# Placing every on-chip tile that TensorE reads at a multiple of 128 bytes

## The chip, the cores and the metric

The kernel runs on one core of a Trainium2 chip. The metric is device time in microseconds (us); lower is better. Names of engines in the profile: PE is TensorE's matmul stream, PEld its weight loads, DVE is VectorE, ACT is ScalarE, POOL is GpSimd, SP is the engine that issues nearly all DMAs here.

## What is computed

Talking-heads attention over 8 batches, 12 heads, 448 tokens and head size 64, then a feed-forward layer over 3584 tokens with 768 inputs, 2048 hidden values and 768 outputs. All of it is in fp32; the weights of the second part arrive as float64.

```python
scores = scale * np.matmul(q, k.transpose(0, 1, 3, 2))
scores = np.einsum('bhij,hg->bgij', scores, w_pre)
attn = np.exp(scores - np.max(scores, axis=-1, keepdims=True))
attn = attn / (np.sum(attn, axis=-1, keepdims=True) + 1e-09)
attn = np.einsum('bhij,hg->bgij', attn, w_post)
x = np.matmul(attn, v)          # then heads are joined: 3584 x 768
h = x @ w_in
out = (h - np.tanh(h)) @ w_out
```

## The kernel before

**Two stages.** The first stage is attention. It goes over 32 blocks (8 batches, each of three times 120 tokens and once 88) and over 180 places; a place handles two groups of up to 10 tokens by 12 heads, so 120 rows. At each place `gather` (L487) brings two groups of scores from the tile `s` into tiles `t` by DMA, `split` makes a high and a low float32r part of one group (`th` on DVE at L495, `tl` on POOL at L496), `premix` multiplies by the 120x120 matrix `wpre` (L503, fp32, shown as two records) or by its two parts `wph` and `wpl` (L506 to L508, float32r), `expo` takes maximum and exponential (L518 on DVE, L520 on ACT), `norm` scales `wpost` by the row sums into `wr` (L536 on ACT), and `mix` multiplies the exponentials `e` as weights by `wr` as moving operand (L548), which ACT copies into `at` (L557, L564). Beside this, at places that a small planner picks, `prep_q` transposes queries (L432) and writes them as `qh` on ACT (L445) and `ql` on DVE (L447), `prep_k` does the same for keys (`kk`), `scores` multiplies the two (L466) and `values` multiplies `at` by the values `vr` (L585). The feed-forward weights are narrowed from float64 in the same stage.

The second stage is the feed-forward layer: 7 batches of 512 tokens by 16 slices of 128 hidden values, 112 steps. A step has 18 matmuls of 512 columns in `hidden` (L246, L247, L251: a 128x128 piece of `w` as weights, `xh` or `xl` as moving operand), and for each of four token tiles 3 matmuls of 512 and 3 of 256 columns in `result` (L290, L291, L293: a 128x128 piece of `gh` or `gl` as weights, `w` as moving operand). ACT and DVE do the gate (`gate`, L261 to L271) and its two parts (L278, L279). Weights come through a ring of six tiles, `w0` to `w2` in a pool on the left and `w3` to `w5` in one on the right.

**What sets the order.** Each engine's instructions stand in the order in which the Python code emits them (`in_order`); `sooner`, `then` and `last` put the copies of a place behind its matmuls.

**Where tiles lie.** Pools are stacked from the left end of on-chip memory upwards and from the right end downwards, and every tile starts at a multiple of 32 bytes. No tile is placed by hand, so a small tile moves all that is stacked behind it. With this kernel the left stack of the first stage begins at a multiple of 128, and the two buffers of `qh` and of `ql` (2880 bytes a partition each) break it by 64; the right stack is 96 bytes past a multiple of 128 throughout, since the small tiles of `cst` and the ring of `wr` (960 bytes a buffer) are no whole multiples; and in the second stage the 8-byte tile `bias` puts all that lies behind it on the left 32 bytes past. First bytes, modulo 128, of what TensorE reads:

| read at | moving operand | weights |
|---|---|---|
| L246, L247, L251 | `xh`, `xl`: 0 | `w0` to `w2`: 32; `w3` to `w5`: 96 |
| L290, L291, L293 | `w0` to `w2`: 32; `w3` to `w5`: 96 | `gh`, `gl`: 32 |
| L466 | `kk`: 0 | `qh`, `ql`: 0, 32, 64 and 96, by head pair and buffer |
| L503 | `t`: 96 | `wpre`: 96 |
| L506, L507, L508 | `th`, `tl`: 96 | `wph`: 32, `wpl`: 0 |
| L548 | `wr`: 0, 32, 64, 96 | `e`: 96, 32 |
| L585 | `at`: 0, 32, 64, 96 | `vr`: 96 |
| L406, L432 | `ident`: 96 | `ko`, `qr`: 0 |

Of the kernel before, what the change touches and what calls it, by code (L numbers as in the profile page):

```python
# [10 lines left out]
F32 = mybir.dt.float32  # L11
F32R = mybir.dt.float32r
# [9 lines left out]
def raw(ap):  # L22

    return ap.bitcast(F32)
# [5 lines left out]


CW = 512


def narrow_steps(nc, pool, dma, chunks):
# [5 lines left out]
    def load(src):  # L41
        p, n2 = src.shape
        r = pool.tile([p, CW, 2], I32, name="cr", tag="cr", bufs=3)[:, : n2 // 2]
        return r, dma(r.rearrange("p n t -> p (n t)"), src)
# [23 lines left out]
def narrow_chunk(nc, pool, dma, r, dst):  # L68
    p, n, _ = r.shape
    hi, lo = r[:, :, 1], r[:, :, 0]  # L70
    m = pool.tile([p, CW], F32, name="cm", tag="cm", bufs=2)[:, :n]
    s = pool.tile([p, CW], I32, name="cs", tag="cs", bufs=2)[:, :n]
    u, w = hi, lo
# [23 lines left out]
    fh = s.bitcast(F32R)  # L97
    fl = pool.tile([p, CW], F32R, name="cl", tag="cl", bufs=2)[:, :n]
    nc.scalar.copy(fh, m)
# [46 lines left out]
def kernel_body(  # L146
# [11 lines left out]
    nc = tc.nc  # L158
    B, H, S, D = q.shape
    P = 128  # L160
    DM = H * D
    DF = w_in.shape[1]
    NP = H // 2
# [3 lines left out]
    MT = GI * H  # L167
    GP = GI * H
# [32 lines left out]
    ff = SimpleNamespace(w={}, x={}, raw={}, out={})  # L201

    def open_early():
        def pool(name, bufs):
            return ctx.enter_context(tc.tile_pool(name=name, bufs=bufs, side="left", reuse_waits="tile"))

        ff.xp, ff.w0 = pool("xp", 2 * NK), pool("w0", 1)
        ff.rw, ff.gp = pool("rw", 1), pool("gpool", 3)
        ff.bias = ff.w0.tile([P, 2], F32, name="bias", tag="bias")
        nc.gpsimd.memset(ff.bias[:, 0:1], GATE_A[1])  # L210
        nc.gpsimd.memset(ff.bias[:, 1:2], GATE_B[1])

    def open_ps_h():
        ff.ps_h = ctx.enter_context(tc.tile_pool(name="ps_h", bufs=2, space=PSUM, side="left"))

    def open_late():
        ff.wp = ctx.enter_context(tc.tile_pool(name="wp", bufs=1, side="right", reuse_waits="tile"))
        ff.op = ctx.enter_context(tc.tile_pool(name="op", bufs=4, side="right", reuse_waits="tile"))
        ff.ps_y = ctx.enter_context(tc.tile_pool(name="ps_y", bufs=1, space=PSUM, side="left"))
# [100 lines left out]
    with ExitStack() as st:  # L320

        early, early_ps = ctx.enter_context(ExitStack()), ctx.enter_context(ExitStack())
        ld = early.enter_context(tc.tile_pool(name="ld", bufs=2, side="left"))
        sp = early.enter_context(tc.tile_pool(name="sp", bufs=2, side="left"))
        cv = early.enter_context(tc.tile_pool(name="cv", bufs=1, side="left"))
        cst = st.enter_context(tc.tile_pool(name="cst", bufs=1, side="right"))
        kp = st.enter_context(tc.tile_pool(name="kp", bufs=1, side="right"))
        gp = st.enter_context(tc.tile_pool(name="gp", bufs=4, side="right"))
# [95 lines left out]
        def prep_q(i, t):  # L424

            n = sizes[blocks[i][1]]
            assert sent[i, "q"]()
            ps = ps_m.tile([P, 512], F32, name="ps_m", tag="ps_m")
            pv = ps[:, : 3 * MT].rearrange("p (r i) -> p r i", r=3)
            for r in range(3):  # L430
                hp = 3 * t + r
                nc.tensor.transpose(  # L432
                    pv[:, r, :n], qrs[i][:n, 2 * hp : 2 * hp + 2, :].rearrange("p h d -> p (h d)"), ident[:n, :n]
                )
            pv = pv[:, :, :n]

            def rest():
                if t == 0:
                    qbs[i] = [
                        ld.tile([P, NP * MT], F32R, name=x, tag=x)[:, : NP * n].rearrange("p (h i) -> p h i", i=n)  # L440
                        for x in ("qh", "ql")
                    ]
                qh, ql = qbs[i]
                tt = slice(3 * t, 3 * t + 3)
                nc.scalar.mul(qh[:, tt], pv, scale)  # L445
                then.append(
                    lambda: nc.vector.scalar_tensor_tensor(  # L447
                        out=ql[:, tt], in0=pv, scalar=scale, in1=raw(qh[:, tt]), op0=ALU.mult, op1=ALU.subtract
                    )
                )  # L450
                if t == 1:
                    del qrs[i]

            sooner.append(rest)

        def scores(i, hp, engines=None):
# [68 lines left out]

        def norm(p):
            zs = te[p][1]
            wr = gp.tile([GP, 2, GP], F32, name="wr", tag="wr", bufs=2)
            n0, n1 = rows[2 * p], rows[2 * p + 1]
            for j, n in enumerate((n0, n1)):  # L530

                nc.vector.tensor_scalar_add(zs[:n, 1, j : j + 1], zs[:n, 0, j : j + 1], 1e-9)
            for js, n in ((slice(0, 2), n0),) if n0 == n1 else ((slice(0, 1), n0), (slice(1, 2), n1)):
                nc.vector.reciprocal(zs[:n, 2, js], zs[:n, 1, js])
            for j, n in enumerate((n0, n1)):
                nc.scalar.mul(wr[:n, j, :], wpost[:n, :], zs[:n, 2, j : j + 1])  # L536
            te[p].append(wr)
# [120 lines left out]
        )  # L658
        ps_w = ps_s[:GP, 1, : 2 * H].rearrange("p (w g) -> p w g", w=2)
        nc.tensor.matmul(ps_w.rearrange("p w g -> p (w g)"), repeat, w12.rearrange("p w g -> p (w g)"), start=True, stop=True)  # L660
        wpre = cst.tile([GP, GP], F32, name="wpre")
        wpost = cst.tile([GP, GP], F32, name="wpost")
        pre_v = wpre.rearrange("p (i g) -> p i g", i=GI)
        post_v = wpost.rearrange("p (g i) -> p g i", i=GI)
        nc.vector.tensor_copy(pre_v, ps_w[:, 0, :].unsqueeze(1).to_broadcast([GP, GI, H]))
# [12 lines left out]
        def scores_0(hq):  # L678
            for hp in (2 * hq, 2 * hq + 1):
                scores(0, hp, (nc.scalar.copy, nc.vector.tensor_copy))  # L680
                sooner.pop()()
# [9 lines left out]
        prep_q(1, 1)  # L691
        flush()
        scores_0(2)
        wph = cst.tile([GP, GP], F32R, name="wph")
        wpl = cst.tile([GP, GP], F32R, name="wpl")
        nc.vector.tensor_copy(wph, wpre)
        nc.vector.tensor_sub(wpl, wpre, raw(wph))
        now()
# [35 lines left out]
        at_s, p, kind = {}, 0, None  # L734
        while halved:
            ready = sorted((x for x in halved if x[0] <= p), key=lambda x: (x[1], x[3:]))
            if ready:
                x = ready[0]
# [3 lines left out]
                if x[2] == kind and other and x[1] > p + 1:  # L742
                    x = other[0]
                halved.remove(x)
                _, _, kind, i, n = x
# [7 lines left out]
        for i, (b, m) in enumerate(blocks):  # L753
            p0 = first[i] // 2
            if i + 2 < len(blocks):
                p = at_s[i + 2, 0] - 1
# [7 lines left out]
        for b in range(1, B):  # L764
            p, o = first[blocks.index((b - 1, 1))] // 2 - 1, 0
            for hq in range(3):
                at_place(p, load_k, b, hq)
                p = o = max(p + 2, o)
# [26 lines left out]
        for p in range(NPL + 3):  # L795
# [13 lines left out]
            if 1 <= p < NPL + 1:  # L809
                norm(p - 1)  # L810
# [20 lines left out]
            if p == NPL - 3:  # L831
                conv.rest(now)
                early.close()
                open_early()
# [6 lines left out]


    open_late()
    ahead = RING - 1
    for n in range(EARLY, ahead):
# [53 lines left out]
```

## Time and profile before

| what | value |
|---|---|
| median of three timed runs | 1901.55 us (1899.92 to 1905.39) |
| the profiled execution | 1894.16 us, of which the span of its instructions is 1892.4 us |
| PEld busy | 1528.4 us, 81% |
| DVE busy | 1191.6 us, 63% |
| ACT busy | 1138.7 us, 60% |
| POOL busy | 484.0 us, 26% |
| DMA | 371.92 MB at 197 GB/s on average |
| TensorE clock granted | 0.997 of full speed |

The profile is of one execution, which was 7.4 us under the median of the timed runs. A matmul's record begins when it is issued; its end is modelled, and records of neighbouring matmuls overlap. So the time that a matmul takes in a full stream is read from the distance between the beginnings of neighbouring records, not from the duration in a record. An fp32 matmul has two records, a float32r matmul has one, and a transpose one. A group's row gives the line, engine, operation, tiles and shapes, then its count, its busy time and the mean duration of one, and the idle time before it with what ended it.

### The profile page before, as it was taken

The page shows a single profiled execution, that of the slowest core. Times are in us where ns is not written, and L with a number is a line of the kernel's source. Part 1 is how long each engine was busy: PE and PEld are TensorE (multiplying, and loading weights), DVE is VectorE, ACT ScalarE, POOL GpSimd, SP SyncE. Part 2 cuts the span into 40 slices and gives each one's busy share as a digit, 9 for nine tenths or more (in the row PEclk, how much of TensorE's full clock was granted, in tenths as well). Part 3 has the DMA queues.
Part 4 walks back from the last instruction along what each step waited for, and adds up shares of the span by engine and source line. Part 5 has one row for each costly group of instructions (what it writes and reads, how often), then busy time and mean ns, then how long its engine had stood idle before and what let it go on. Part 6 is the DMA issues. An engine that isn't in the chain of part 4 may idle for free.

```text
span 1892.4 us, 35415 instructions
## 1 busy us (share of the span) xinstructions
PE 1864.3 (99%) x13154; PEld 1528.4 (81%) x13154; DVE 1191.6 (63%) x2464; ACT 1138.7 (60%) x2513; POOL 484.0 (26%) x442
## 2 busy tenths in 40 slices
PE   7999999999999999999999999999999999999998
PEld 5787887877888788787788888888888888888887
DVE  4676766777776686776455565555555555556555
ACT  4887888878888688888634434444444443443433
POOL 1454545444554355544200000010000000010000
PEclk9999999999999999999999999999999999999999
DMA  5567658675665757656565555655656655555550
GB/s 137 181 192 211 189 159 235 180 213 181 195 213 156 208 178 206 204 159 183 194 268 207 210 212 212 226 200 214 218 199 217 215 207 209 212 213 201 214 197 34
DMA packets 199963, 371.92 MB, mean 197 GB/s; under 512 B 55920, under 2 KB 174704, under 8 KB 185456
## 3 DMA queue, kind: packets, MB, share of 16 engines
q1 hardware_dynamic: 199744, 369.67, 59.5%
q8 instruction: 104, 1.70, 0.4%
q14 instruction: 67, 0.55, 0.1%
q10 hardware_dynamic: 48, 0.00, 0.0%
HBM read 245.37 MB, written 47.19 MB: 155 GB/s over the span
## 4 chain that ended last, share of the span: by engine, by line
PE 88%; DMA 5%; ACT 2%; DVE 2%; issue 1%; POOL 1%; SPq 1%; ACTq 0%; POOLq 0%; DVEq 0%
PE ps_o L548 14%; PE ps_h L251 8%; PE ps_h L247 8%; PE ps_h L246 8%; PE ps_m L585 7%; PE ps_q L466 6%; PE ps_p L503 6%; PE ya L290 5%; PE ya L291 5%; PE ya L293 5%; PE yb L291 3%; PE yb L293 3%; PE yb L290 3%; DMA t<-s 2%; PE ps_p L508 2%; PE ps_p L507 2%
## 5 line engine op out<-in xcount | busy, mean ns | idle before, releaser
L548 PEld LDWEIGHTS ps_o<-wr,e 120*112 120x112 f32 (+1 forms) x2880 | 307.6, 177 | 48.7 <-issue 30.6
L548 PE MATMUL ps_o<-wr,e 120*112 120x120 f32 (+1 forms) x2880 | 340.7, 272 | 4.1 <-ACT wr L536 4.1
L518 DVE TENSOR_REDUCE mx<-ps_p 120x1 f32<-120x448 f32 x360 | 218.6, 622 | 134.3 <-PE ps_p L503 134.0
L278 ACT CAST gh<-r 128x512 fp32r<-128x512 f32 (+1 forms) x113 | 69.7, 617 | 381.7 <-DVE r L271 381.7
L496 POOL TENSOR_TENSOR tl<-t,th 120x448 fp32r<-120x448 f32 (+1 forms) x180 | 206.2, 1146 | 355.8 <-DVE th L495 221.3
L247 PE MATMUL ps_h<-xl,w 128*128 128x512 f32 x672 | 266.2, 396 | 0.5 <-POOL xl L236 0.5
L246 PE MATMUL ps_h<-xh,w 128*128 128x512 f32 x672 | 266.1, 396 | 0.0
L236 POOL TENSOR_TENSOR xl<-rx,xh 128x512 fp32r<-128x512 f32 x38 | 57.7, 1519 | 745.8 <-ACT xh L235 745.8
L520 ACT ACTIVATE e<-ps_p,mx 120x448 f32<-120x448 f32 x360 | 226.0, 637 | 31.6 <-DVE mx L518 31.3
L557 ACT COPY at<-ps_o 112x960 f32<-112x960 f32 x156 | 154.6, 991 | 108.2 <-PE ps_o L548 107.5
L290 PE MATMUL ya<-w,gh 128*128 128x512 f32 x448 | 177.4, 396 | 2.5 <-ACT gh L278 2.5
L267 DVE SCALAR_TENSOR_TENSOR r<-qa,ps_h 128x512 f32<-128x512 f32 (+1 forms) x113 | 77.2, 684 | 159.9 <-ACT t L264 159.9
L291 PE MATMUL ya<-w,gh 128*128 128x512 f32 x448 | 177.1, 395 | 0.0
L293 PE MATMUL ya<-w,gl 128*128 128x512 f32 x448 | 175.4, 392 | 0.7 <-DVE gl L279 0.7
L251 PE MATMUL ps_h<-xh,w 128*128 128x512 f32 x672 | 175.1, 396 | 0.0
L503 PE MATMUL ps_p<-t,wpre 120*120 120x448 f32 x360 | 165.7, 542 | 3.2 <-ACT e L520 2.3
L585 PE MATMUL ps_m<-at,vr 112*64 112x120 f32 (+1 forms) x3072 | 163.5, 264 | 3.6 <-ACT at L564 2.9
L585 PEld LDWEIGHTS ps_m<-at,vr 112*64 112x64 f32 x3072 | 149.8, 138 | 17.0 <-ACT at L564 5.4
L261 ACT ACTIVATE u<-ps_h 128x512 f32<-128x512 f32 (+1 forms) x113 | 67.2, 595 | 159.8 <-PE ps_h L251 159.7
L251 PEld LDWEIGHTS ps_h<-xh,w 128*128 128x128 f32 x672 | 126.3, 188 | 30.6
L247 PEld LDWEIGHTS ps_h<-xl,w 128*128 128x128 f32 x672 | 126.5, 188 | 26.7 <-POOL xl L236 1.3
L246 PEld LDWEIGHTS ps_h<-xh,w 128*128 128x128 f32 x672 | 126.5, 188 | 25.4
(92 smaller groups left out, 3660.5 us busy)
## 6 DMA issues: line engine op xcount, KB each, us to landing
w<-ws SPq DMA_DIRECT2D x112, 1536.0 KB
t<-s SPq DMA_DIRECT2D x344, 210.0 KB
cr<-in_moe_w_in_dram SPq DMA_DIRECT2D x24, 512.0 KB
cr<-in_moe_w_out_dram SPq DMA_DIRECT2D x32, 384.0 KB
vr<-in_v_dram SPq DMA_DIRECT2D x24, 448.0 KB
out_dram<-ob SPq DMA_DIRECT2D x28, 384.0 KB
kr<-in_k_dram SPq DMA_DIRECT2D x21, 448.0 KB
qr<-in_q_dram SPq DMA_DIRECT2D x23, 360.0 KB
```

Of the source, the lines that this page charges most:

```text
L246: nc.tensor.matmul(ph, wh[:, fs], xh, start=(c == 0), stop=False)
L247: nc.tensor.matmul(ph, wh[:, fs], xl, start=False, stop=False)
L251: nc.tensor.matmul(ph, wl[:, fs], xh, start=False, stop=(c == NK - 1))
L290: nc.tensor.matmul(y, gh[:, tok], wh[:, es], start=first, stop=False)
L291: nc.tensor.matmul(y, gh[:, tok], wl[:, es], start=False, stop=False)
L293: nc.tensor.matmul(y, gl[:, tok], wh[:, es], start=False, stop=last)
L496: nc.gpsimd.tensor_sub(tl[:n, :], x[:n, :], raw(th[:n, :]))
L503: nc.tensor.matmul(pa[:n, :], wpre[:n, :n], tg.pop(2 * p)[:n, :], start=True, stop=True)
L518: nc.vector.tensor_reduce(out=mx[:n, :], in_=ps[:n, :], axis=AX.X, op=ALU.max, negate=True)
L520: nc.scalar.activation(e[:n, :], ps[:n, :], AF.Exp, bias=mx[:n, :], scale=1.0, accum_out=zs[:n, 0, j : j + 1])
L548: nc.tensor.matmul(ps[:CP, j, c * GP : (c + 1) * GP], e[:n, c * CP : (c + 1) * CP], wr[:n, j, :], start=True, stop=True,)
L585: nc.tensor.matmul(pv[j * D : (j + 1) * D, r, :n], vt[:, j, c, :], ats[i][:, c, 2 * hp + j, :n], start=(c == 0), stop=(c == NC - 1),)
```

## The change

`bias` gets a whole line of 128 bytes, 2 of its 32 columns used. A pad of 96 bytes is opened at the right end of memory ahead of the right stack of each stage, and filled by a memset on POOL. The two buffers of `qh` and of `ql` hold six rows of 128 columns, of which the first 120 or 88 are used, in place of six rows close together. `wr` and the four 120x120 matrices get rows of 128 columns, of which 120 are used.

```diff
+LINE = 32
...
-        ff.bias = ff.w0.tile([P, 2], F32, name="bias", tag="bias")
+        ff.bias = ff.w0.tile([P, LINE], F32, name="bias", tag="bias")
...
+    def rest_of_line(stack):
+
+        pad = stack.enter_context(tc.tile_pool(name="pad", bufs=1, side="right"))
+        nc.gpsimd.memset(pad.tile([P, LINE - 8], F32, name="pad", tag="pad"), 0.0)
+
     def open_late():
+        rest_of_line(ctx)
         ff.wp = ctx.enter_context(tc.tile_pool(name="wp", bufs=1, side="right", reuse_waits="tile"))
...
+        rest_of_line(st)
         cst = st.enter_context(tc.tile_pool(name="cst", bufs=1, side="right"))
...
                     qbs[i] = [
-                        ld.tile([P, NP * MT], F32R, name=x, tag=x)[:, : NP * n].rearrange("p (h i) -> p h i", i=n)
+                        ld.tile([P, NP, P], F32R, name=x, tag=x)[:, :, :n]
                         for x in ("qh", "ql")
                     ]
...
-            wr = gp.tile([GP, 2, GP], F32, name="wr", tag="wr", bufs=2)
+            wr = gp.tile([GP, 2, P], F32, name="wr", tag="wr", bufs=2)[:, :, :GP]
...
-        wpre = cst.tile([GP, GP], F32, name="wpre")
-        wpost = cst.tile([GP, GP], F32, name="wpost")
+        wpre, wpost = [cst.tile([GP, P], F32, name=x)[:, :GP] for x in ("wpre", "wpost")]
...
-        wph = cst.tile([GP, GP], F32R, name="wph")
-        wpl = cst.tile([GP, GP], F32R, name="wpl")
+        wph, wpl = [cst.tile([GP, P], F32R, name=x)[:, :GP] for x in ("wph", "wpl")]
```

With it every operand in the table above begins at a multiple of 128, with two exceptions. The second and fourth piece of `e`, a weight at L548, begin at 64, since a piece is 448 bytes long. `at` still has rows of 480 bytes, so the moving operand of L585 begins at 0, 32, 64 or 96 as before. Destinations of DMAs into `t`, `vr`, `w` and `rx` move to multiples of 128 with their tiles.

The order on PE, DVE, ACT and SP is the same row by row, and so are the semaphores that each instruction waits for. POOL gets two memsets. The first stands ahead of the identity matrix at the start of the program; before:

```order
L883 MEMSET const-uint8-127 128x1
L894 UNCONDITIONAL_BRANCH
masks.py:197 MEMSET ident 128x128
masks.py:199 ISA
masks.py:199 AFFINE_SELECT ident<-ident 128x128
L654 MEMSET tmp_w 12x120
```

and now, with the new line numbers:

```order
L891 MEMSET const-uint8-127 128x1
L902 UNCONDITIONAL_BRANCH
L222 MEMSET pad 128x24
masks.py:197 MEMSET ident 128x128
masks.py:199 ISA
masks.py:199 AFFINE_SELECT ident<-ident 128x128
L664 MEMSET tmp_w 12x120
```

So the pad's memset is queued ahead of the identity matrix, which the first matmuls read. The second one stands on POOL where the second stage opens, among the subtractions that make the low parts `xl` of the tokens; before:

```order
L210 MEMSET bias 128x1
L211 MEMSET bias 128x1
L496 TENSOR_TENSOR tl<-t,th 108x448
L236 TENSOR_TENSOR xl<-rx,xh 128x512 x38
L894 UNCONDITIONAL_BRANCH
```

and now:

```order
L213 MEMSET bias 128x1
L214 MEMSET bias 128x1
L506 TENSOR_TENSOR tl<-t,th 108x448
L245 TENSOR_TENSOR xl<-rx,xh 128x512 x2
L222 MEMSET pad 128x24
L245 TENSOR_TENSOR xl<-rx,xh 128x512 x36
L902 UNCONDITIONAL_BRANCH
```

The first batch's two subtractions are ahead of the memset, the 36 of the later batches behind it. On ACT and DVE the only difference is the shape of the query parts; on ACT before:

```order
L445 ACT_TABLE_LOAD
L445 ACTIVATE qh<-ps_m 128x360 x2
L397 COPY tmp_o<-vr 112x2x4x64 x2
L417 CAST kk<-ps_m 128x448 x4
L472 COPY s<-ps_q 120x448 x2
```

and now:

```order
L455 ACT_TABLE_LOAD
L455 ACTIVATE qh<-ps_m 128x3x120 x2
L407 COPY tmp_o<-vr 112x2x4x64 x2
L427 CAST kk<-ps_m 128x448 x4
L482 COPY s<-ps_q 120x448 x2
```

One write of 360 columns in a row is now three of 120 with a gap of 8 columns between them, and the same holds for `ql` on DVE.

## The prediction

> **What bounds the kernel now.** I read the page first: its busy shares, and the shares of the chain of work that ended last. Then the table of busy time by stretch, cut where attention ends (950 us).
>
> ```profile
> span 1892.4 us, 35415 instructions
> PE 1864.3 (99%) x13154; PEld 1528.4 (81%) x13154; DVE 1191.6 (63%) x2464; ACT 1138.7 (60%) x2513; POOL 484.0 (26%) x442
> PE 88%; DMA 5%; ACT 2%; DVE 2%; issue 1%; POOL 1%; SPq 1%; ACTq 0%; POOLq 0%; DVEq 0%
> 50.00:950.00 900.00, 890.98 (x8242) 715.60 (x8242) 627.03 (x1620) 733.23 (x1809) 419.55 (x388) 1.00 0.64 191
> 950.00:1875.00 925.00, 924.28 (x4624) 775.29 (x4623) 536.18 (x775) 375.13 (x635) 55.02 (x36) 1.00 0.58 207
> ```
>
> The last two rows give the stretch, its length, then busy time of PE, PEld, DVE, ACT and POOL, the granted clock, the DMA share and GB/s. PE is idle for 900.00 - 890.98 = 9.0 us of attention and 925.00 - 924.28 = 0.7 us of the feed-forward stage, and the clock is 1.00 in both. So **TensorE's own stream sets the end**, and a change of layout can move the time by much only if it changes the time from one matmul to the next. All else that the change could speed up is worth at most the idle 9.7 us.
>
> **Does the place of an operand change a matmul's time?** Before, the tiles lie at different places modulo 128, so the trace holds the comparison already. I look at the beginnings of neighbouring matmuls in the timeline. First the feed-forward stage; the stretch 1400.89 to 1401.95 reads `w5` (moving, 96 past a line) with `gh`, `gl` as weights (32 past); from 1401.95 on the moving `xh`, `xl` lie at 0 and the weights `w1` at 32.
>
> ```profile
> 1400.89 0.40 PE L290 MATMUL ya<-w,gh 128*128 128x512 f32 x1
> 1401.13 0.40 PE L291 MATMUL ya<-w,gh 128*128 128x512 f32 x1
> 1401.36 0.39 PE L293 MATMUL ya<-w,gl 128*128 128x512 f32 x1
> 1401.59 0.28 PE L290 MATMUL yb<-w,gh 128*128 128x256 f32 x1
> ...
> 1401.95 0.39 PE L246 MATMUL ps_h<-xh,w 128*128 128x512 f32 x1
> 1402.18 0.40 PE L247 MATMUL ps_h<-xl,w 128*128 128x512 f32 x1
> 1402.41 0.40 PE L246 MATMUL ps_h<-xh,w 128*128 128x512 f32 x1
> 1402.64 0.40 PE L247 MATMUL ps_h<-xl,w 128*128 128x512 f32 x1
> ```
>
> With the moving operand off a line, three matmuls of 512 columns go from 1400.89 to 1401.59: 0.233 us each. With it on a line, three go from 1401.95 to 1402.64: 0.230 us each. The three of 256 columns between 1401.59 and 1401.95 take 0.12 us each, half of it, so the time goes by columns, and no cost per weight load shows that a better placed weight could take away.
>
> In this stage weights never begin on a line, so I go to attention for that. In the first rows below `th` and `tl` (96 past) move against `wpl` (L507, on a line) and `wph` (L508, 32 past). In the second rows keys `kk` (on a line) move in pairs against queries: 70.39 to 71.10 is one pair of heads with its weights on a line, 71.10 to 71.80 the next, whose weights are 96 past.
>
> ```profile
> 300.22 1.01 PE L503 MATMUL ps_p<-t,wpre 120*120 120x448 f32 x2 [0.30 <-ACT e L520]
> 300.84 0.59 PE L506 MATMUL ps_p<-th,wph 120*120 120x448 f32 x1
> 301.27 0.36 PE L507 MATMUL ps_p<-th,wpl 120*120 120x448 f32 x1
> 301.48 0.36 PE L508 MATMUL ps_p<-tl,wph 120*120 120x448 f32 x1
> 301.68 0.62 PE L432 MATMUL ps_m<-ident,qr 88*128 88x88 f32 x6
> ```
>
> ```profile
> 70.39 0.67 PE L466 MATMUL ps_q<-kk,qh 64*120 64x448 f32 x4
> 70.89 0.37 PE L466 MATMUL ps_q<-kk,ql 64*120 64x448 f32 x2
> 71.10 0.57 PE L466 MATMUL ps_q<-kk,qh 64*120 64x448 f32 x4
> 71.50 0.37 PE L466 MATMUL ps_q<-kk,ql 64*120 64x448 f32 x2
> 71.80 1.89 PE L548 MATMUL ps_o<-wr,e 120*112 120x120 f32 x16
> ```
>
> L507 takes 301.48 - 301.27 = 0.21 us, L508 takes 0.20 us. The pair at 70.89 has both operands on a line and takes 0.21 us for 448 columns; the two pairs from 71.10 to 71.50, weights off a line, take 0.20 us each. A head pair is 0.71 us in the one case and 0.70 us in the other; the longer gap of about 0.3 us stands once in each, where the engine enters the half-height matmuls (70.39) and where it leaves them (71.80). So **placed well or badly, moving or as weights, a matmul takes the same**, and the first term, 112 feed-forward steps and 180 places of attention, is 0.
>
> The Trainium skill speaks for this: SBUF — State Buffer, section Specifications (TRN2), gives on-chip memory lines of 16 bytes, by which every tile here was at the start of a line before. The rows above agree.
>
> **The other engines and the DMAs** write and read the moved tiles too. Nearest rows: ACT writes `gh` (32 past) and `xh` (on a line) from tiles 32 past; DVE reads and writes `gl` (32 past), and `xl` (on a line).
>
> ```profile
> L278 ACT CAST gh<-r 128x512 fp32r<-128x512 f32 x111 | 68.9, 621 | 376.7 <-DVE r L271 376.7
> L235 ACT CAST xh<-rx 128x512 fp32r<-128x512 f32 x42 | 25.7, 622 | 19.6 <-DMA rx<-xs 19.4
> L279 DVE TENSOR_TENSOR gl<-r,gh 128x512 fp32r<-128x512 f32 x111 | 77.6, 699 | 77.2 <-ACT gh L278 77.2
> L236 DVE TENSOR_TENSOR xl<-rx,xh 128x512 fp32r<-128x512 f32 x4 | 2.6, 688 | 2.3 <-ACT xh L235 2.3
> DVE th L495 <- DMA t<-s: 50.3, 23, 5.6
> ```
>
> 621 against 622 ns and 699 against 688 ns: no gain on an engine. The destination of the gathers into `t` goes from 96 past to a line. No row prices that alone; DVE waited 50.3 us for them in all, 23 times (last row), but PE, behind them, was idle for only 9.0 us from 50 to 950 us. So the gain of faster landings lies between 0 and 9.0 us; I take 0, since TensorE's rows show next to nothing to win.
>
> **What is added.** Two pad memsets on POOL, and a gap in the rows of `qh` and `ql`.
>
> ```profile
> L210 POOL MEMSET bias<- 128x1 f32 x1 | 0.1, 105 | 0.0
> 10.44 0.76 DVE L397 COPY tmp_o<-vr 112x512 f32<-112x512 f32 x2 [1.65 <-DMA vr<-in_k_dram]
> L236 POOL TENSOR_TENSOR xl<-rx,xh 128x512 fp32r<-128x512 f32 x38 | 57.7, 1519 | 745.8 <-ACT xh L235 745.8
> L445 ACT ACTIVATE qh<-ps_m 128x360 fp32r<-128x360 f32 x48 | 20.3, 489 | 4.3 <-PE ps_m L432 4.2
> L447 DVE SCALAR_TENSOR_TENSOR ql<-ps_m,qh 128x360 fp32r<-128x360 f32 x48 | 23.3, 527 | 11.9 <-ACT qh L445 11.5
> L603 DVE COPY x<-ps_m 128x360 f32<-128x360 f32 x48 | 38.0, 791 | 22.6 <-PE ps_m L585 17.8 <-DMA xs<-x 4.6
> ```
>
> A memset of a column takes 0.1 us, one of 24 columns hardly more. The first delays the identity matrix, and with it the first matmuls and the first queries, by 0.1 us; DVE then waits for keys until 10.44 us with 1.65 us idle, which covers it. Without that cover it would cost 0.1 us. The second waits for nothing, and nothing waits for it; only the later subtractions L236 are behind it, on a POOL that waited 745.8 us for ACT ahead of them. Both: 0 to 0.2 us, taken as 0.
>
> The gap turns 64 writes on ACT (48 of 360 columns, 16 of 264) and as many on DVE into three pieces each. No row shows just that. The lower end is 0, the length of a write being the same. The upper end is the difference to L603, which writes the same 360 columns on DVE in a finer scatter: 791 - 527 = 264 ns, so 64 x 0.264 = 16.9 us of work, on each of the two engines. I take 0: the gap of 32 bytes is nearer to L447 than to L603's scatter. The cover, if it does cost: from 50 to 950 us ACT is idle 900 - 733 = 167 us, over 180 places 0.93 us a place, and DVE 273 us, 1.5 us a place; two such writes fall in one place of each block and bring at most 0.53 us.
>
> **The sum.** 0 (TensorE) + 0 (landings, -9.0 at best) + 0 (memsets, +0.2 at worst) + 0 (gaps, +16.9 at worst): the profiled time stays 1894.2 us. The median of the timed runs lies 7.4 us above that execution, so I carry the median of 1901.55 over as 1901.5 us.
>
> **Rivals.**
>
> Faster, by lines: if the engine's time went by lines of 128 bytes touched, 512 columns (16 lines) off a line would touch 17, 448 would touch 15 for 14, and 256 columns 9 for 8. `result` would gain 112 x (12 x 0.233 / 17 + 12 x 0.12 / 9) = 36 us, and premix, which goes from 300.22 to 301.68, 180 x 1.46 / 15 = 17.5 us: 1894.2 - 53.5 = 1841, or 1848 as a median (L548, left out here, would add to it). For it: the diff moves just these operands. Against it: 0.233 beside 0.230 us above. A case with both operands on a line at 128 rows and 512 columns isn't in the trace, only at 64 rows; so 5 in 100. The Trainium skill has a figure that a reader could set beside this: TensorE: Matmul & The Clock Gate, section "Wait — 56ns, not 53.3ns?", states 215.7 ns from one 512-column matmul to the next. If placement were all that keeps these at 233 ns, an estimate from that page, with 109 ns for 256 columns, is 112 x (30 x 17 + 12 x 9) ns = 69 us less. The rows on a line speak against it: they are no nearer to the page's figure.
>
> Faster, by waits: gathers land sooner and the idle 9.0 us of attention goes: 1885, or 1892 as a median. Against it: the wait of TensorE is mostly for ACT, whose instructions don't change. 8 in 100.
>
> Slower, by the gaps: the writes of `qh` cost 0.26 us more each. ACT does them behind a place's exponentials and ahead of the next `wr`, for which L548 waits. It decides where the two writes exceed ACT's slack in that place, 0.53 against 0.93 us on average; if no place had slack, 32 x 0.53 = 17 us: 1911, or 1918 as a median. Where half the places have none, 1910. 13 in 100, for other losses by layout too, such as two engines that now meet at the same place in a line; the pair at 70.89, both operands on a line, shows no such loss.
>
> That the change doesn't do all it says holds in part: `at` and half of `e` stay off a line. By the rows above that costs nothing, so it is in the forecast.
>
> **How the numbers follow.** A measurement of this kernel can tell about 0.3%, 5.7 us, from no change. The forecast, no effect, has 74 in 100; faster 5 + 8 = 13; slower 13. The range takes in the idle time as a gain, 1901.5 - 9.0 - 2.5 = 1890 with the spread of the runs, and the price of the gaps, 1918.
>
> **What would show it.** Right: 512-column matmuls at 0.23 us in both halves of a step, 256 at 0.12, the stretch from 950 to 1875 us with PE idle under 1 us, and the span within some 3 us of 1892.4. L445 and L447 show the price of the gaps: near 489 and 527 ns, or up to 264 ns more. The forecast is wrong if those distances in `result` or `hidden` fall toward 0.22 us (lines), if PE's idle time in attention shrinks from 9 us to near nothing (waits), or if it grows with `wr` (gaps).

## The result and the profile after

The changed kernel takes 1889.8 us (median of 6 runs, 1888.92 to 1891.94), the kernel before 1901.38 us beside it (6 runs, 1899.71 to 1905.71): a ratio of 0.9943, 95% interval 0.9929 to 0.9956. That is 0.57% faster, clear of the 0.3% that can be told. The forecast was no change, and the range's lower end, 1890.0 us, stands 0.2 us above the median; by the ratio, 1901.55 x 0.9943 = 1890.7 us, the time lies just inside the range. Either way the likeliest case was wrong, and small gains that I had priced at 0 came in.

First the page of the changed kernel and its table by stretch, in the columns explained with the prediction:

```profile
span 1888.7 us, 35417 instructions
PE 1859.9 (98%) x13154; PEld 1530.4 (81%) x13154; DVE 1190.8 (63%) x2464; ACT 1137.5 (60%) x2513; POOL 483.1 (26%) x444
PE 89%; DMA 4%; ACT 2%; DVE 1%; issue 1%; SPq 1%; POOL 0%; ACTq 0%; POOLq 0%; DVEq 0%
```

```profile
50.00:950.00 900.00, 890.78 (x8251) 716.33 (x8249) 626.84 (x1619) 733.06 (x1810) 419.94 (x390) 1.00 0.63 191
950.00:1875.00 925.00, 924.16 (x4647) 779.75 (x4646) 536.49 (x777) 377.39 (x642) 54.85 (x36) 1.00 0.58 207
```

TensorE is as busy as before in both stretches. It issues 4647 matmuls where it issued 4624 in the last 925 us, but that tells little: the stretch begins in the tail of attention, and the count moves with the end of attention. The groups of the 512-column matmuls tell more; here the three of `hidden` and the third of `result` before, then all six after (mean duration of a record behind the busy time):

```profile
L247 PE MATMUL ps_h<-xl,w 128*128 128x512 f32 x672 | 266.2, 396 | 0.5 <-POOL xl L236 0.5
L246 PE MATMUL ps_h<-xh,w 128*128 128x512 f32 x672 | 266.1, 396 | 0.0
L251 PE MATMUL ps_h<-xh,w 128*128 128x512 f32 x672 | 175.1, 396 | 0.0
L293 PE MATMUL ya<-w,gl 128*128 128x512 f32 x448 | 175.4, 392 | 0.7 <-DVE gl L279 0.7
```

```profile
L256 PE MATMUL ps_h<-xl,w 128*128 128x512 f32 x672 | 263.8, 393 | 0.5 <-POOL pad L222 0.5
L255 PE MATMUL ps_h<-xh,w 128*128 128x512 f32 x672 | 263.8, 393 | 0.0
L299 PE MATMUL ya<-w,gh 128*128 128x512 f32 x448 | 177.5, 396 | 2.6 <-ACT gh L287 2.6
L300 PE MATMUL ya<-w,gh 128*128 128x512 f32 x448 | 177.2, 396 | 0.0
L302 PE MATMUL ya<-w,gl 128*128 128x512 f32 x448 | 176.3, 393 | 0.6 <-DVE gl L288 0.6
L260 PE MATMUL ps_h<-xh,w 128*128 128x512 f32 x672 | 172.9, 392 | 0.0
L222 POOL MEMSET pad<- 128x24 f32 x2 | 0.2, 118 | 0.3 <-POOLq L891 0.3
L455 ACT ACTIVATE qh<-ps_m 128x360 fp32r<-128x360 f32 x48 | 20.3, 490 | 4.9 <-PE ps_m L442 4.8
L457 DVE SCALAR_TENSOR_TENSOR ql<-ps_m,qh 128x360 fp32r<-128x360 f32 x48 | 23.3, 527 | 12.0 <-ACT qh L455 11.9
```

`hidden` lost 396 - 393 = 3 or 4 ns a matmul, busy time 266.2 + 266.1 + 175.1 - (263.8 + 263.8 + 172.9) = 6.9 us in all. `result` won nothing; its third group is 0.9 us busier. The last three rows settle the added work: a pad's memset is 118 ns, and the gaps in `qh` and `ql` cost nothing (490 and 527 ns beside 489 and 527). The 0.5 us of waiting that the row of L256 puts down to the pad was put down to `xl` before.

The gain in `hidden` isn't spread evenly. The timeline of the changed kernel, cut to the first record of two stretches of `hidden` and to the first of `result` behind each; the first stretch has its weights in `w2`, the second in `w3`:

```profile
1408.99 0.39 PE L255 MATMUL ps_h<-xh,w 128*128 128x512 f32 x1
...
1413.17 0.40 PE L299 MATMUL ya<-w,gh 128*128 128x512 f32 x1
...
1417.38 0.39 PE L255 MATMUL ps_h<-xh,w 128*128 128x512 f32 x1
...
1421.48 0.39 PE L299 MATMUL ya<-w,gh 128*128 128x512 f32 x1
```

The 18 matmuls take 4.18 us from `w2` and 4.10 us from `w3`. All tiles here lie at multiples of 128. What tells the two apart is the offset modulo 256: `xh` and `xl` begin at 128, `w0` to `w2` at 0, and `w3` to `w5` at 128.

The whole stage can be read from the view of the tile `ya`, which gives the first and the last start of L290 (now L299) over 112 steps; before and after:

```profile
L290 PE MATMUL ya<-w,gh x448: 387/396/502, 951.6 to 1886.4; 128*128 128x512 f32 x150
```

```profile
L299 PE MATMUL ya<-w,gh x448: 387/396/505, 952.5 to 1882.7; 128*128 128x512 f32 x150
```

1886.4 - 951.6 = 934.8 us before, 1882.7 - 952.5 = 930.2 us after: 4.6 us less. The beginnings of the records split this: added up over the trace from the first start of `result` to the last step's, from the first record of a step's `hidden` to the first of the `result` behind it and on to the next `hidden`, `hidden` takes 462.8 us before and 455.9 us after, 6.9 us less, and `result` 461.7 and 464.0 us, 2.3 us more. The medians differ by 11.6 us, so something is missing from this pair of profiles. The profiled execution before took 1894.2 us, less than any of its six timed runs; the one after, 1890.5 us, lies among its own. The rest of the gain is therefore looked for in attention, over more executions.

### The profile page after: what moved, and what is told of

Same layout as the page of the kernel before. It is cut to its first block, busy times and chain, and to the rows that moved or that the text cites. A ratio compares the mean times of both kernels' runs of the same rounds, so it can differ in the third digit from the quotient of the medians.

```text
span 1888.7 us, 35417 instructions
## 1 busy us (share of the span) xinstructions
PE 1859.9 (98%) x13154; PEld 1530.4 (81%) x13154; DVE 1190.8 (63%) x2464; ACT 1137.5 (60%) x2513; POOL 483.1 (26%) x444
## 3 DMA queue, kind: packets, MB, share of 16 engines
q1 hardware_dynamic: 199744, 369.67, 59.2%
## 4 chain that ended last, share of the span: by engine, by line
PE 89%; DMA 4%; ACT 2%; DVE 1%; issue 1%; SPq 1%; POOL 0%; ACTq 0%; POOLq 0%; DVEq 0%
PE ps_o L558 15%; PE ps_h L260 8%; PE ps_h L256 8%; PE ps_h L255 8%; PE ps_m L595 8%; PE ps_q L476 6%; PE ps_p L513 6%; PE ya L299 5%; PE ya L300 5%; PE ya L302 5%; PE yb L300 3%; PE yb L302 3%; PE yb L299 3%; DMA t<-s 2%; PE ps_p L517 2%; PE ps_p L516 2%
## 5 line engine op out<-in xcount | busy, mean ns | idle before, releaser
L256 PE MATMUL ps_h<-xl,w 128*128 128x512 f32 x672 | 263.8, 393 | 0.5 <-POOL pad L222 0.5
L255 PE MATMUL ps_h<-xh,w 128*128 128x512 f32 x672 | 263.8, 393 | 0.0
L299 PE MATMUL ya<-w,gh 128*128 128x512 f32 x448 | 177.5, 396 | 2.6 <-ACT gh L287 2.6
L260 PE MATMUL ps_h<-xh,w 128*128 128x512 f32 x672 | 172.9, 392 | 0.0
L256 PEld LDWEIGHTS ps_h<-xl,w 128*128 128x128 f32 x672 | 126.4, 188 | 24.8 <-POOL pad L222 0.9
```

The costliest lines, as they stand in the source:

```text
L255: nc.tensor.matmul(ph, wh[:, fs], xh, start=(c == 0), stop=False)
L256: nc.tensor.matmul(ph, wh[:, fs], xl, start=False, stop=False)
L260: nc.tensor.matmul(ph, wl[:, fs], xh, start=False, stop=(c == NK - 1))
L299: nc.tensor.matmul(y, gh[:, tok], wh[:, es], start=first, stop=False)
```

## The experiments

Three batches, each timed against the kernel before on its own chip, 5 rounds. **Theory F** puts the gain into the pace of `hidden`, **theory A** into attention.

| kernel | median, us | ratio to before | 95% interval | feed-forward stage, us |
|---|---|---|---|---|
| ctl_before | 1900.11 | 1.0005 | 0.9993 to 1.0016 | 934.8 |
| ff_only | 1895.84 | 0.9981 | 0.9971 to 0.9991 | 930.5 |
| attn_only | 1893.54 | 0.9970 | 0.9960 to 0.9981 | 934.8 |
| all128 | 1885.42 | 0.9929 | 0.9915 to 0.9943 | 925.7 |
| pad_only | 1894.22 | 0.9975 | 0.9964 to 0.9986 | 934.5 |
| gaps_only | 1898.29 | 0.9998 | 0.9989 to 1.0007 | 934.0 |
| x_at_0 | 1890.74 | 0.9959 | 0.9946 to 0.9971 | 930.3 |
| s_at_0 | 1878.22 | 0.9895 | 0.9881 to 0.9908 | 925.0 |
| s_only | 1892.19 | 0.9958 | 0.9945 to 0.9970 | 934.2 |
| all256 | 1878.67 | 0.9888 | 0.9875 to 0.9901 | 925.0 |
| changed_again | 1889.33 | 0.9950 | 0.9937 to 0.9963 | 930.4 |

The last column is read as above, from the first start to the last start of the first line of `result`, in the one profiled execution of each kernel.

### ctl_before: the kernel before, unchanged

> The kernel before once more, unchanged, to see how far one profiled execution of it lies from its timed runs. If the 7 us between the first profile (1894.2 us) and the median (1901.4 us) are differences between executions, this profile's hidden and result stretches of the feed-forward stage add up to another sum than 943.9 us, and its span lies nearer to 1900 us. If the first profile was typical, the span is again within 2 us of 1892.4 us. Ratio to before 1.000 within 0.15%.

The view of `ya`, the table by stretch and the waits of this second profile of the same program:

```profile
L290 PE MATMUL ya<-w,gh x448: 387/396/502, 956.3 to 1891.1; 128*128 128x512 f32 x150
```

```profile
50.00:950.00 900.00, 887.71 (x8193) 712.43 (x8193) 624.16 (x1615) 732.38 (x1809) 420.13 (x389) 1.00 0.63 191
```

```profile
DVE th L495 <- DMA t<-s: 58.1, 24, 6.1
```

The span is 1897.1 us. The feed-forward stage is again 934.8 us, so I expected the difference between executions in the wrong stage: it lies in attention, which ends 4.7 us later (956.3 against 951.6). TensorE is idle for 12.3 us of the stretch from 50 to 950 us in place of 9.0, and DVE waits 58.1 us for the gathers in place of 50.3. So the bound of 9.0 us that I drew from one profile was itself one draw.

### ff_only and attn_only: one stage each

```diff
-        ff.bias = ff.w0.tile([P, 2], F32, name="bias", tag="bias")
+        ff.bias = ff.w0.tile([P, 32], F32, name="bias", tag="bias")
...
     def open_late():
+        rest_of_line(ctx)
```

> Only the feed-forward stage's tiles are moved to multiples of 128 (the line for bias, and the pad at the right end when that stage opens); attention lies as before. Theory F (the gain is TensorE's pace in the 18 matmuls of hidden, by where weights lie): all of the gain is here, ratio 0.994 to 0.995, hidden at w3 to w5 4.10 us in place of 4.21 us. Theory A (the gain is in attention): ratio 1.000, and hidden unchanged.

> Only attention's tiles are moved (the pad under the first right stack, the query parts, wr and the four 120x120 matrices in rows of 128); the feed-forward stage lies as before. Theory F: ratio 1.000 within 0.1%, feed-forward stretches as before. Theory A: ratio near 0.995.

`attn_only` is the rest of the change: the pad under the first right stack, and the query parts, `wr` and the four matrices in rows of 128. The groups of `hidden` in `ff_only`, and in `attn_only`:

```profile
L253 PE MATMUL ps_h<-xl,w 128*128 128x512 f32 x672 | 263.8, 393 | 0.5 <-POOL pad L219 0.5
L252 PE MATMUL ps_h<-xh,w 128*128 128x512 f32 x672 | 263.8, 393 | 0.0
```

```profile
L255 PE MATMUL ps_h<-xl,w 128*128 128x512 f32 x672 | 266.2, 396 | 0.5 <-POOL xl L244 0.5
L254 PE MATMUL ps_h<-xh,w 128*128 128x512 f32 x672 | 266.1, 396 | 0.0
```

Neither theory alone holds. The feed-forward part is worth 0.19% and the attention part 0.30%; together 0.9981 x 0.9970 = 0.9951, within the interval of the whole change (0.9929 to 0.9956).

### all128 and x_at_0: what sets the pace of hidden

```diff
-        ff.bias = ff.w0.tile([P, LINE], F32, name="bias", tag="bias")
+        ff.bias = ff.w0.tile([P, 2 * LINE], F32, name="bias", tag="bias")
```

> As the changed kernel, but bias takes 256 bytes, so that all that lies behind it on the left moves by 128 more: w0 to w2, gh and gl then begin 128 past a multiple of 256, as xh, xl and w3 to w5 do in the changed kernel already. Theory D (the pace goes by the distance between weights and moving operand modulo 256): hidden takes 4.10 us at all six weight tiles, result 4.20 us at all six, and the feed-forward stage is about 7 us shorter than in the changed kernel (56 x 0.09 + 56 x 0.03). Theory L (whole lines of 128 are all that counts): no change against the changed kernel, within 1 us.

The timeline of `all128`, first at weights in `w2`, then in `w3`:

```profile
1406.14 0.40 PE L255 MATMUL ps_h<-xh,w 128*128 128x512 f32 x1
...
1410.24 0.39 PE L299 MATMUL ya<-w,gh 128*128 128x512 f32 x1
...
1414.47 0.40 PE L255 MATMUL ps_h<-xh,w 128*128 128x512 f32 x1
...
1418.57 0.39 PE L299 MATMUL ya<-w,gh 128*128 128x512 f32 x1
```

Both take 4.10 us now. The feed-forward stage falls from 930.2 to 925.7 us, 4.5 us, not the 7 us that theory D promised: summed as above, `hidden` goes from 455.9 to 452.2 us, 3.7 us less, where 5.0 were promised (56 x 0.09), and `result` from 464.0 to 463.2 us, where 1.7 were promised (56 x 0.03). `result` stays longer than the 461.7 us before the change. Theory L, that whole lines of 128 are all that counts, falls, for every tile lay on one before.

In both quick cases so far, `w3` to `w5` in the changed kernel and all six in `all128`, both operands lie 128 past a multiple of 256, and that may be what counts (theory S). So `x_at_0` moves `xh` and `xl` and leaves the weights where the changed kernel has them, modulo 256:

```diff
+        lp = ctx.enter_context(tc.tile_pool(name="lp", bufs=1, side="left"))
+        nc.gpsimd.memset(lp.tile([P, LINE], F32, name="lp", tag="lp"), 0.0)
         ff.xp, ff.w0 = pool("xp", 2 * NK), pool("w0", 1)
...
-        ff.bias = ff.w0.tile([P, LINE], F32, name="bias", tag="bias")
+        ff.bias = ff.w0.tile([P, 2 * LINE], F32, name="bias", tag="bias")
```

> As the changed kernel, but with 128 bytes ahead of xp and 256 for bias, so that modulo 256 xh and xl begin at 0, w0 to w2 at 0 (as in the changed kernel), w3 to w5 at 128 (as there), gh and gl at 0. Theory D (the distance between weights and moving operand modulo 256 sets the pace of hidden): hidden turns round, 4.10 us at w0 to w2 and 4.18 to 4.21 us at w3 to w5. Theory S (hidden is quick where both lie 128 past a multiple of 256): 4.18 us or more at all six. Theory R (it is where w3 to w5 lie in memory, not their offset): w3 to w5 stay at 4.10 us, w0 to w2 at 4.18 us.

Its timeline, again at `w2` and then at `w3`:

```profile
1411.74 0.40 PE L257 MATMUL ps_h<-xh,w 128*128 128x512 f32 x1
...
1415.84 0.39 PE L301 MATMUL ya<-w,gh 128*128 128x512 f32 x1
...
1420.07 0.39 PE L257 MATMUL ps_h<-xh,w 128*128 128x512 f32 x1
...
1424.25 0.39 PE L301 MATMUL ya<-w,gh 128*128 128x512 f32 x1
```

4.10 us at `w2`, 4.18 us at `w3`: the two have changed places, and theories S and R fall. Weights whose offset didn't change became quick or slow as the moving operand moved. So `hidden` goes by **the distance between weights and moving operand modulo 256**: taken over all steps of one weight tile, the median is 4.09 to 4.11 us at a distance of 0, 4.18 to 4.20 at 128, and, as before the change, 4.20 to 4.21 at 32 (`w0` to `w2`) and 4.21 to 4.22 at 96 (`w3` to `w5`).

### pad_only and gaps_only: what in attention gains

```diff
+        rest_of_line(st)
         cst = st.enter_context(tc.tile_pool(name="cst", bufs=1, side="right"))
```

> Of attention's edits only the 96-byte pad under the right stack: t, th, tl, e, at, vr and x begin at multiples of 128, while wpost, wph, wpl, the second half of wr and half of qh and ql stay off a line; the feed-forward stage lies as before. Theory G (attention's gain is DMA: data that lands in or leaves on-chip memory at a multiple of 128 takes the DMA engines less time, so gathers land sooner): nearly the whole gain of attn_only, ratio 0.9965 to 0.998, DVE waits for the gathers 45 to 50 us. Theory P (it is TensorE's reads of the padded operands): ratio 0.999 to 1.000.

> The rest of attention's edits without that pad: query parts, wr and the four 120x120 matrices in rows of 128 columns, the right stack still 96 past a line. Theory G: no change, ratio 1.000 within 0.1%, DVE waits for the gathers 50 us or more; the writes of qh and ql on ACT and DVE keep their 489 and 527 ns within 10 ns. Theory P: ratio near 0.997.

`gaps_only` is `attn_only` without that line. First the wait and the DMA queue of `pad_only`, then the wait of `gaps_only`, then its writes of the query parts:

```profile
DVE th L501 <- DMA t<-s: 46.8, 21, 5.9
q1 hardware_dynamic: 199744, 369.67, 59.0%
```

```profile
DVE th L503 <- DMA t<-s: 49.7, 24, 5.7
```

```profile
L455 DVE SCALAR_TENSOR_TENSOR ql<-ps_m,qh 128x360 fp32r<-128x360 f32 x48 | 23.3, 526 | 11.6 <-ACT qh L453 11.4
L453 ACT ACTIVATE qh<-ps_m 128x360 fp32r<-128x360 f32 x48 | 20.2, 488 | 3.8 <-PE ps_m L440 3.7
```

The pad alone has 0.9975, nearly all of the 0.9970 of `attn_only`; the padded rows have 0.9998. So in attention the operands of TensorE that were given whole lines bring nothing. What brings the gain is the move of the right stack. DMAs land there (`t`, `vr`) and leave (`x`), and TensorE reads `t`, `e`, `wr`, `vr` and `wpre` there, among others. The two costliest matmul groups that read them are no quicker, before and in the changed kernel:

```profile
L548 PE MATMUL ps_o<-wr,e 120*112 120x120 f32 (+1 forms) x2880 | 340.7, 272 | 4.1 <-ACT wr L536 4.1
L503 PE MATMUL ps_p<-t,wpre 120*120 120x448 f32 x360 | 165.7, 542 | 3.2 <-ACT e L520 2.3
```

```profile
L558 PE MATMUL ps_o<-wr,e 120*112 120x120 f32 (+1 forms) x2880 | 340.1, 271 | 3.7 <-ACT wr L546 3.7
L513 PE MATMUL ps_p<-t,wpre 120*120 120x448 f32 x360 | 165.6, 542 | 3.1 <-ACT e L530 2.3
```

Busy time differs by 0.6 and 0.1 us, far from the 0.25% of `pad_only`, 4.7 us. Nor could the distance between two operands do it there: apart from the transposes, attention's matmuls have both in one stack, which the pad moves as a whole, and the transposes, which have one in each, are busy for 22.8 (L432) and 20.0 us (L406) before, 22.8 and 20.2 in `pad_only`. The waits point to the DMAs: DVE waits 50.3, 58.1, 58.4 and 49.7 us for the gathers with the right stack 96 past a line (the first profile, `ctl_before`, `ff_only`, `gaps_only`), and 45.9 to 48.2 us in the six profiles with it on a line and `s` where it was (`pad_only` above, and the changed kernel here):

```profile
DVE th L505 <- DMA t<-s: 48.2, 21, 5.6
```

The DMA queue says the same more sharply: its share of the span, as a time of all 16 engines, comes to 1123 to 1128 us in those four profiles and 1112 to 1118 us in the six. How this shortens the kernel is argued, not shown: from 50 to 950 us TensorE is idle for 8.7 to 14.5 us in the four and 7.3 to 10.6 us in the six, 9.8 us in `pad_only`, so a single pair of profiles can't show a gain of 4.7 us there.

### s_at_0, s_only and all256: the other end of the gathers

If the place where a gather lands matters, so may the place it is read from. The score tile `s` lies 128 past a multiple of 256 in both kernels. 128 bytes under the first left stack move it, and all else in that stack, to a multiple of 256:

```diff
+        lp = early.enter_context(tc.tile_pool(name="lp", bufs=1, side="left"))
+        nc.gpsimd.memset(lp.tile([P, 32], F32, name="lp", tag="lp"), 0.0)
         ld = early.enter_context(tc.tile_pool(name="ld", bufs=2, side="left"))
```

`s_at_0` is `all128` with this, `s_only` the kernel before with this and nothing else. `all256` has it with `x_at_0`, and a late pad of 224 bytes, so that `w3` to `w5` begin at 0 too.

> As all128, with 128 bytes ahead of the first stage's left stack, so that the score tile s, the source of the gathers, begins at a multiple of 256 and not 128 past one. If reads cost less from a multiple of 256, a gather's 1792 bytes a row start one line earlier, DVE's wait for gathers falls by several us, and the time falls by 2 to 4 us against all128. If a line of 128 is enough for reads, the time stays within 1 us of all128. The feed-forward stage is that of all128.

> The kernel before with one edit: 128 bytes ahead of the first stage's left stack, so that the score tile s, the source of the gathers, and the other tiles there begin 0 in place of 128 past a multiple of 256. The right stack stays off a line (t at 96), the feed-forward stage as before. If reads from a multiple of 256 are cheaper by themselves: the DMA queue's share falls by about 1% of the span, DVE waits for gathers 38 to 46 us, ratio 0.9965 to 0.998. If it needs the destinations on a line too: ratio 0.999 to 1.000.

> Every tile of the left and right stacks that a matmul or a large DMA uses begins at a multiple of 256 (only ident and the four 120x120 matrices lie 128 past). Theory D gives hidden 4.10 us at all six weight tiles, as in s_at_0, since the distance between weights and moving operand is 0 modulo 256 again; theory S, that both must lie 128 past a multiple of 256, gives 4.18 us or more. By theory D the time is within 2 us of s_at_0, 1878 us.

> The changed kernel once more, beside the other two on this chip. Ratio to before 0.993 to 0.996; 8 to 14 us above s_at_0 and all256.

The wait for the gathers and the DMA queue of the kernel before (its queue's row alone, the wait stands in the prediction), of `s_only` and of `s_at_0`:

```profile
q1 hardware_dynamic: 199744, 369.67, 59.5%
```

```profile
DVE th L497 <- DMA t<-s: 47.6, 25, 4.7
q1 hardware_dynamic: 199744, 369.67, 58.4%
```

```profile
DVE th L507 <- DMA t<-s: 39.6, 20, 4.6
q1 hardware_dynamic: 199744, 369.67, 58.1%
```

The same 369.67 MB take the 16 DMA engines 59.5% of 1892.4 us before, that is 1126 us, and 58.4% of 1890.1 us in `s_only`, 1104 us. `s_only` alone (0.9958) is nearly as much as the whole change, though no operand of TensorE changes its offset modulo 128 in it, and the feed-forward stage stays at 934.2 us. It gained more than the 0.9965 to 0.998 that I expected, while the wait for the gathers, 47.6 us, fell less than expected. The effects add: `s_at_0` waits 39.6 us for the gathers and has 0.9895, near 0.9929 x 0.9958 = 0.9887; its queue comes to 58.1% of 1880.2 us, 1092 us. Against `all128`, on another chip, it is 7.2 us faster, more than the 2 to 4 us that I expected.

But the reading of `s` is a small part of the fall in DMA time, 22 us. Added up by packet size in the traces, as a time of the 16 engines, packets of 1792 bytes, nearly all gathers, took 234.5 us before and 232.2 us in `s_only`. Packets of 256 bytes, which are nearly all queries on their way into `qr` in the same stack, took 59.2 and 51.7 us, and packets of 1024 bytes, nearly all keys and values, 93.5 and 89.3 us. In `pad_only` the three come to 231.2, 57.9 and 91.7 us: there the gathers gain most of the three.

`all256` has 0.9888 and a feed-forward stage of 925.0 us with both operands at 0 modulo 256, as theory D has it. It and `s_at_0` can't be told apart. Against `changed_again` on the same chip all256 is 1889.33 - 1878.67 = 10.7 us faster. So **both beat the two kernels of this case**, at about 1.1% under the kernel before.

## Why the prediction was wrong where it was

**TensorE's pace, taken as 0.** This step failed. It compared rows that differ in where one operand lies, found 0.233 beside 0.230 us and 0.21 beside 0.20, and concluded that placement does nothing. Two things were wrong with it. The effect is 3.4 ns of 233 (6.9 us over the 2016 matmuls of `hidden`), under the 10 ns to which a timeline's beginnings are printed; what could have shown it is a sum over a whole stage, 56 steps or more. And the comparison looked at each operand's own offset from a line. `all128` and `x_at_0` show that the distance between the two operands counts; none of the pairs that I lined up at 128 rows had that distance at 0. I had noted that this case was missing, and gave it 5 in 100 with a mechanism (lines touched) that the runs refute: it promised 36 us in `result`, which got 2.3 us longer. The term measures -4.6 us, -6.9 in `hidden` and +2.3 in `result`.

**Landings, taken as 0 between 0 and -9.0 us.** The bounds held, the choice didn't: `pad_only` shows 0.25%, 0.0025 x 1898.6 = 4.7 us. The reason I gave, that TensorE's rows show next to nothing to win, rested on one execution, and on TensorE's waits for ACT. But ACT's work stands behind the gathers through DVE and TensorE, so that unchanged instructions on ACT were no reason. The rival "by waits", at 8 in 100, is nearest to what gave about half of the gain, in that the DMAs got shorter. The sign I had named for it, TensorE's idle time in attention near nothing, didn't come: 900.00 - 890.78 = 9.2 us after, 9.0 us before.

**Memsets and gaps, taken as 0.** Right: 118 ns each and hidden, and 490 and 527 ns for the writes; `gaps_only` at 0.9998 confirms it as a whole. The slower rival, 17 us, had no price at all.

**The profiled execution.** I carried "no change" from one profile over to the median. The profile before was 7.4 us under its median, which I noted and did not ask about. `ctl_before` shows that attention differs by 4.7 us between two executions of one program.

**The range.** Its lower end was the whole idle 9.0 us and 2.5 us of spread. The time came out next to it by another sum, 4.6 us of TensorE's pace and 4.7 us or so in attention; that the two nearly meet is luck.

What stays open: which of the moved ends in attention counts (the landing of `t`, that of `vr`, or the reading of `x`; in `s_only` the reading of `s`, or the landing of keys and queries), since a pad moves a whole stack: the packets show which transfers got shorter, not which of them the kernel was waiting for. A gap that moves one tile alone wasn't tried. Nor was a distance of 64 in `hidden`, or a reason found why `result` doesn't follow the rule of `hidden`: with `w0` to `w2` its operands lay at distance 0 modulo 256 before the change already, at 4.19 to 4.20 us a step, and with all six in `all128`, where it takes 4.18 to 4.23 us.

## What to carry to other kernels

Ask of each placement who reads or writes the tile: here a multiple of 128 was the wrong goal for TensorE, whose matmuls in `hidden` went quicker when weights and moving operand lay at the same offset modulo 256 (those in `result` didn't). For tiles that DMAs read or fill it paid to move a stack from 96 past a multiple of 128 onto one, and another from 128 past a multiple of 256 onto one. Padding the rows of small operands brought nothing; such a pad of 96 or 128 bytes under a stack brought 0.25% and 0.42%. An effect of 1 or 2% on a matmul is not seen in single rows: sum a stage, and profile the same program twice before a few microseconds are called no change.

## What the runs showed of the hardware

In `hidden`, a stream of 512-column float32r matmuls with 128x128 weights ran at 4.10 / 18 = 0.228 us each with the two operands at the same offset modulo 256, and 4.18 / 18 = 0.232 to 4.21 / 18 = 0.234 us at the other distances tried. The Trainium skill, TensorE: Matmul & The Clock Gate, section "Step-by-step: what each phase is for", states two independent read ports, so that loading weights doesn't take bandwidth from a running matmul; a pace in `hidden` that depends on the distance between the two operands is hard to square with that, though how they meet wasn't shown. Its DMA: Bandwidth & Descriptors, section "How a descriptor splits into AXI transactions", has reads that don't begin at a multiple of 256 bytes pay for the bytes ahead: a gather's row of 1792 bytes from 128 past a boundary would be an estimated 60 beats in place of 56. `s_only` agrees in direction only: the packets of 1792 bytes went from 234.5 to 232.2 us, 1%, where the beats would give 7%. Most of the 22 us by which its DMA time fell, 1126 to 1104 us, is in other transfers, first of all in the queries, whose landing place moved and not the place they are read from; of those the sentence on reads says nothing.
